# A transformer block in fp32 on one core: layer norm scales of the late half spread by products with the identity, second half's operands split later

## The chip, the core and the metric

The kernel runs on one core of a Trainium2 chip: TensorE (PE) for matmuls, VectorE (DVE), ScalarE (ACT) and GpSimd (POOL) for the rest, and SyncE (SP), which here does nothing but issue DMAs. Each engine takes its instructions in the order of the program and waits, where it must, for semaphores that others raise. The metric is the device time of one execution in microseconds.

## The reference, cut to what matters

```python
x = A_x                                   # 2048 x 1024
h = x + A(layernorm(x), wqkv, w_phi, wo)  # linear attention, 32 heads of 32
h2 = h + relu(layernorm(h) @ w1) @ w2     # w1 1024 x 3584, w2 3584 x 1024
```
A projects to q, k and v, maps q and k per head through w_phi and two softmaxes, sums phi_k^T v and phi_k over all rows, divides, and multiplies by wo. All is fp32. layernorm has no weights: (x - mean) / sqrt(var + 1e-5).

## The kernel before, in words

**Precision.** Each fp32 operand of a large product is split into a high part (`fp32r`, a ScalarE copy) and a low part (the difference, on VectorE or GpSimd), and one product becomes three matmuls, lines L182 to L184 (`mm3`): high by high, high by low, low by high. Three matmuls of 128x512 are one *step*.

**Stages.** In order of the program: the key/value and query projections, the attention, its output projection (`wo`, 32 items of 8 steps: 16 tiles of 128 rows, 2 halves of columns), the up product of the MLP and the down product. Both MLP products are done by a Strassen-like scheme with seven products m in the order 1, 5, 6, 2, 7, 3, 4 (`UP`). The rows come in two halves b = 0 and 1 of 1024. An item (b, p, m) of the up product is 4 steps (12 matmuls); its left operand is a block of w1 (a *unit*), its right one is `hT[m]`, a 128x4x512 operand in a high and a low part, used by 14 items of one half and then overwritten for the other half.

**Where `hT` comes from.** The rows h of tile t are stored to memory (`hd`) by `wo_store` (L688), and their layer norm has two ways. For the first half (*near*, `ln_pair`, i = 0 to 3, two tiles each) a tile is loaded, normed on ScalarE (L239), transposed on TensorE (L246, L715) and copied back by ScalarE (L248, L716); the seven sums are stored to `hs` (L734). The steps of each pair stand in the table `NEAR`. For the second half (*far*, `far_stats`, `far_pair`, table `FAR`) the statistics of each tile are taken as its rows are finished; `ln_power` makes from them two numbers a row (factor and offset, L231 to L233, GpSimd). The rows are loaded later with rows and columns exchanged in another pattern, so that a partition needs the scales of another row: `far_scale` (L748) stores them, four copies of each pair, into memory (`scd`), `far_pair` stage 2 loads them back (L763) into `scx`, and stage 3 norms with them (L769).

**Loading and splitting `hT`.** `h_load` loads `hs` into the low part (L804 for b = 0, L808 for b = 1: g = 0, 1 are the halves of the 512 columns; for b = 1 four DMAs each), `h_high` splits off the high part on ScalarE (L816), `h_low` subtracts on VectorE (L820).

**The up product's results.** After the items m = 1, 5, 6 ScalarE copies the bank (L843, `up_take`), since m = 6, 7, 3, 4 go on summing in a bank that was used before (`BANK_OF`): m = 7 in the bank of m = 6, m = 3 in that of m = 5. VectorE adds (L846, L852, L855), ScalarE takes the relu (L849), and SP stores (L858, `ad`).

**Weights.** The class `Units` loads units (L338, six slots `raw`) and splits them (L125 on ScalarE, L129 on VectorE or GpSimd, ten slots `w`) some steps ahead; a load waits for a slot, that is, for the split of the sixth unit before.

**What sets the order.** There is no scheduler: `when(step, f, ...)` hangs each piece of work on a step, and the text of the program on every engine follows from this. `up_step(b, p, m)` is the step after item (b, p, m); `up0` is the first step of the up product, `wo0` that of the output projection. SP's queue is in order too, and a DMA that waits holds up all behind it.

Of the kernel before, what the change touches and what calls it, by code (L numbers as in the profile page):

```python
# [9 lines left out]
F32 = mybir.dt.float32  # L10
F32R = mybir.dt.float32r
AF = mybir.ActivationFunctionType
# [3 lines left out]
P = 128  # L16
# [6 lines left out]
HT = NT // 2  # L23
NK = D // P
NC = DFF // P
NP = NC // 2
# [114 lines left out]
def kernel(  # L141
# [12 lines left out]
    v, act, pool, pe, sp = nc.vector, nc.scalar, nc.gpsimd, nc.tensor, nc.sync  # L154
# [4 lines left out]
    lnp = ctx.enter_context(tc.tile_pool(name="lnp", bufs=2))  # L159
    dram = ctx.enter_context(tc.tile_pool(name="scratch", bufs=1, space=bass.MemoryType.DRAM))  # L160
# [6 lines left out]
    def tp_bank():  # L167
        return psum.tile([P, 512], F32, name="tp", bufs=2)
# [20 lines left out]
    def do(n, k, f, *args):  # L189
        at[n, k].append((f, args))  # L190
# [9 lines left out]


    hs = {(b, m): dram.tile([P, 4, 4, P], F32, name=f"hs{b}_{m}") for b in range(2) for m in UP}
    scd = [dram.tile([2, 4 * P * 2], F32, name=f"scd{i}") for i in range(4)]
    ad = {(b, m, p): dram.tile([P, 512], F32, name=f"ad{b}_{m}_{p}")
          for b in range(2) for m in UP for p in range(NP)}
    td = {(w, p): dram.tile([P, 4, 512], F32, name=f"t{w}_{p}") for w in (1, 2) for p in range(NP)}
# [2 lines left out]
    xin, xst, xnt = {}, {}, {}  # L209
# [17 lines left out]
    def ln_power(key):  # L227

        mv = xst[key]
        sc = scx[:, key[1] - HT, 0, :] if key[0] == "s" else lnp.tile([P, 2], F32, name="sc", bufs=4)  # L230
        pool.tensor_scalar_add(sc[:, 0:1], mv[:, 1:2], LN_EPS)  # L231
        pool.tensor_tensor(out=sc[:, 0:1], in0=sc[:, 0:1], in1=half, op=ALU.pow)
        pool.tensor_scalar(sc[:, 1:2], mv[:, 0:1], sc[:, 0:1], -1.0, op0=ALU.mult, op1=ALU.mult)  # L233
        xst[key] = sc
# [501 lines left out]
    def far_stats(t, hf):  # L736
        if hf == 0:
            hst[t] = hp.tile([P, 2, 6], F32, name="hst", bufs=8)
        v.bn_stats(out=hst[t][:, hf, :], in_=xh[t, hf])
        if hf == 1:  # L740
            xst["h", t] = mv = lnp.tile([P, 2], F32, name="mv", bufs=4)
            v.bn_aggr(out=mv, in_=hst.pop(t))

    hst = {}

    def far_scale(t):
        dst = scd[t % 4][t % HT // 4].rearrange("(a p s) -> p a s", a=4, s=2)
        sp.dma_start(dst, xst.pop(("h", t))[:, None, :].to_broadcast([P, 4, 2]))  # L748

    def far_swap(dst, src):  # L750
        v.transpose(dst.rearrange("p (c t g) -> p g c t", c=8, g=4), src.rearrange("p (g c k) -> p g c k", g=4, c=8))

    def far_pair(i, stage):

        tiles = [HT + 4 * r + i for r in range(2)]
        if stage < 2:
            t = tiles[stage]
            xnt["h", t] = x = lnp.tile([P, D], F32, name="xin")
            for a in range(4):
                sp.dma_start(x[32 * a:32 * (a + 1)].rearrange("t (g r f) -> t g r f", g=4, r=2),  # L760
                             hd[t].rearrange("(t g) (r a f) -> a t g r f", g=4, r=2, a=4)[a])
        elif stage == 2:
            sp.dma_start(scx[:, 2 * i:2 * i + 2].rearrange("p r g s -> p r (g s)"),  # L763
                         scd[i].rearrange("r (p f) -> p r f", f=8))
        elif stage == 3:
            for r, t in enumerate(tiles):
                for g in range(4):
                    x, sc = xnt["h", t][:, 256 * g:256 * (g + 1)], scx[:, 2 * i + r, g]
                    act.activation(x, x, AF.Identity, bias=sc[:, 1:2], scale=sc[:, 0:1])  # L769
        elif stage == 4:  # L770
            x1, x2 = (xnt.pop(("h", t)) for t in tiles)
            y2 = mp.tile([P, D], F32, name="y2", bufs=1)
            sums[1, i] = x1, x2, y2
            far_swap(y2, x2)
        elif stage == 5:
            s, y1, y2 = sums[1, i]
            far_swap(y1, s)
        elif stage == 6:
            s, y1, y2 = sums[1, i]
            v.tensor_add(s[:, 0:512], y2[:, 0:512], y2[:, 512:])  # L780
            v.tensor_sub(y2[:, 0:512], y1[:, 0:512], y2[:, 0:512])
        elif stage == 7:
            s, y1, y2 = sums[1, i]
            s4 = mp.tile([P, 512], F32, name="s4l", bufs=1)
            pool.tensor_tensor(out=s[:, 512:], in0=s[:, 0:512], in1=y1[:, 0:512], op=ALU.subtract)
            pool.tensor_tensor(out=s4, in0=y1[:, 512:], in1=s[:, 512:], op=ALU.subtract)
            sums[1, i] = s, y1, y2, s4
# [132 lines left out]
    def item(gen, *args, keys):  # L920
        items.append((gen, args + (keys,)))
        steps.extend((k,) for k in keys)
        return len(items) - 1
# [11 lines left out]
    for b, tiles in enumerate(groups):  # L935
        for hf in range(2):

            pairs = b == 0 and hf == 0
            for j in range(0, 4, 2 if pairs else 1):
# [3 lines left out]
                for half in range(2):  # L943
                    n = item(wo_pair, tiles[j:j + 2], hf, half, keys=[("wo", hf, 4 * half + k // 2) for k in range(8)])
# [36 lines left out]
    for t in range(1, NT):  # L981
        n = t - 1 if t < HT else q_n[1, t - HT] + 1
# [107 lines left out]
    for u in range(32):  # L1090
        start = 8 * (a0 + u) if u >= 8 else 8 * (last_kv + 4) + 19 * u // 2
# [10 lines left out]
        if u < EARLY:  # L1102
            start = 8 * (kv_n[1, u // 2, NT - 1] + 4) + (-2, 19)[u % 2]
# [6 lines left out]
    for (t, hf), n in order:  # L1110
        do(max(n - 1, wo_first), -1, wo_load, t, hf)
        added = 8 * n + (11 if n < wo_first + 2 else 9)
        when(added, wo_add, t, hf)
        if t >= HT:
            when(added, far_stats, t, hf)
            if hf == 1:
                when(added + 4, ln_power, ("h", t))
                when(added + 15, far_scale, t)
        when(8 * n + (10 if n > order[-3][1] else 14), wo_store, t, hf)

    NEAR = {1: (0, 9, 12, 17, 30, 31, 32, 33, 35, 40), 2: (6, 14, 17, 20, 24, 25, 26, 27, 29, 36)}
    FAR = 0, 4, 8, 28, 34, 38, 42, 46, 54
    wo0 = 8 * wo_first
    up0 = 8 * first_up
    for i in range(4):
        near, far = wo0 + 64 + 40 * i, up0 + 60 + 68 * i
        ln2 = NEAR.get(i, (0, 9, 12, 17, 24, 25, 26, 27, 29, 36))
        for stage in range(9):  # L1130
            when(near + ln2[stage], ln_pair, i, stage)
        for stage in range(8):
            when(far + FAR[stage], far_pair, i, stage)
        for j in range(7):
            when(near + ln2[9] + j // 2, ln_store, i, j)
            when(far + FAR[8] + j, far_store, i, j)
    assert wo_n[8, 0] + 10 < first_up

    def up_step(b, p, m):

        return up0 + 4 * (up_n[b, p, m] + 1 - first_up)

    for j, m in enumerate(UP):

        for g in range(2):
            step = up0 + (8 * j + (-62, -32)[g] if j < 4 else 6 * (j - 4) + 10 + 2 * g)
            high = up0 + (8 * j + (-48, -19)[g] if j < 4 else 6 * (j - 4) + 20 + 2 * g)
            when(step, h_load, 0, m, g)
            when(high, h_high, m, g)
            when(high + (2 if j < 4 else 5), h_low, m, g)  # L1150
            step = up_step(0, NP - 1, m) + 3 * j
            when(step + 3 * g, h_load, 1, m, g)
            when(step + 13 + 4 * g, h_high, m, g)
            when(step + 16 + 4 * g, h_low, m, g)

    for b in range(2):
        for p in range(NP):
# [10 lines left out]
    for n, (w, p, j) in enumerate((w, p, j) for w in (1, 2) for p in range(NP) for j in range(2)):  # L1168
        step = sums_at[n]
# [26 lines left out]
    scx = consts.tile([P, HT, 4, 2], F32, name="scx")  # L1196
# [5 lines left out]
    ident = consts.tile([P, P], F32, name="ident")  # L1202
# [9 lines left out]
    for i in range(4):  # L1212
        r = slice(32 * i, 32 * (i + 1))
# [76 lines left out]
```

## Time and profile before

| what | value |
|---|---|
| median of 3 runs | 1899.98 us (1899.32 to 1905.49) |
| the profiled execution | 1903.04 us, span 1901.2 us, mean clock 0.994 |
| TensorE busy | 1877.3 us, 99% |
| VectorE, ScalarE, GpSimd busy | 56%, 39%, 51% |
| DMA | 432.24 MB, mean 227 GB/s |
| DMA queue of SP | 413.43 MB, 71.5% of 16 engines' span |

Times are microseconds from the start of the span. A row of a timeline has the start, the length, the engine, the line, the operation, what is written and read, and in brackets how long the engine stood idle before it and what ended that. In the view of waits stand the total, how often, and the longest. SPq is SP's queue.

### The profile page before, as it was taken

The page shows a single profiled execution, that of the slowest core. Times are in us where ns is not written, and L with a number is a line of the kernel's source. Part 1 is how long each engine was busy: PE and PEld are TensorE (multiplying, and loading weights), DVE is VectorE, ACT ScalarE, POOL GpSimd, SP SyncE. Part 2 cuts the span into 40 slices and gives each one's busy share as a digit, 9 for nine tenths or more (in the row PEclk, how much of TensorE's full clock was granted, in tenths as well). Part 3 has the DMA queues.
Part 4 walks back from the last instruction along what each step waited for, and adds up shares of the span by engine and source line. Part 5 has one row for each costly group of instructions (what it writes and reads, how often), then busy time and mean ns, then how long its engine had stood idle before and what let it go on. Part 6 is the DMA issues. An engine that isn't in the chain of part 4 may idle for free.

```text
span 1901.2 us, 31843 instructions
## 1 busy us (share of the span) xinstructions
PE 1877.3 (99%) x11576; PEld 1538.4 (81%) x11576; DVE 1066.5 (56%) x1695; ACT 738.1 (39%) x1270; POOL 971.7 (51%) x959
## 2 busy tenths in 40 slices
PE   9999999999999999989999989999999999999999
PEld 7877788888788888778888878888888888888887
DVE  7777688677689777445555554334433433343333
ACT  5322244222233122345455554444444444444442
POOL 4887744888847898233233222222244444444443
PEclk9999999999999999999999999999999999999999
DMA  7888788666565666997989997566677677767765
GB/s 225 288 289 293 233 293 256 201 193 198 184 211 162 216 233 214 238 214 230 257 255 260 278 247 231 175 193 198 221 240 217 198 234 236 240 210 221 216 215 178
DMA packets 309261, 432.24 MB, mean 227 GB/s; under 512 B 30192, under 2 KB 171504, under 8 KB 309104
## 3 DMA queue, kind: packets, MB, share of 16 engines
q1 hardware_dynamic: 292208, 413.43, 71.5%
q10 hardware_dynamic: 16896, 16.78, 2.6%
q8 instruction: 91, 1.49, 0.3%
q14 instruction: 66, 0.54, 0.1%
HBM read 292.72 MB, written 137.40 MB: 226 GB/s over the span
## 4 chain that ended last, share of the span: by engine, by line
PE 91%; DMA 5%; POOL 2%; SPq 1%; issue 1%; DVE 1%; ACT 0%; ACTq 0%; POOLq 0%; DVEq 0%
PE mm L182 23%; PE mm L183 23%; PE mm L184 23%; PE ac L184 3%; PE ac L183 3%; PE ac L182 3%; DMA hT<-hs 3%; PE tp L184 2%; PE tp L183 2%; PE tp L182 2%; PE tp L246 1%; PE ac L465 1%; PE tp L634 1%; DMA hd<-xh 1%; POOL w L129 1%; PE ac L634 1%
## 5 line engine op out<-in xcount | busy, mean ns | idle before, releaser
L129 POOL TENSOR_TENSOR w<-raw,w 128x512 fp32r<-128x512 f32 x353 | 468.2, 1328 | 741.8 <-ACT w L125 698.6
L125 ACT ACTIVATE w<-raw 128x512 fp32r<-128x512 f32 x686 | 408.5, 626 | 481.0 <-PE mm L184 230.2
L129 DVE TENSOR_TENSOR w<-raw,w 128x512 fp32r<-128x512 f32 x333 | 271.2, 815 | 522.7 <-ACT w L125 519.3
L182 PE MATMUL mm<-w,xT 128*128 128x512 f32 x768 | 305.4, 398 | 0.0
L183 PE MATMUL mm<-w,xT 128*128 128x512 f32 x768 | 299.9, 390 | 0.7 <-POOL w L401 0.4
L184 PE MATMUL mm<-w,xT 128*128 128x512 f32 x768 | 299.3, 390 | 0.0
L182 PE MATMUL mm<-hT,w 128*128 128x512 f32 x672 | 263.6, 392 | 8.0 <-ACT c L843 4.9
L183 PE MATMUL mm<-hT,w 128*128 128x512 f32 x672 | 263.6, 392 | 3.0 <-DVE hT L820 3.0
L184 PE MATMUL mm<-hT,w 128*128 128x512 f32 x672 | 263.1, 392 | 0.0
L363 POOL TENSOR_TENSOR b<-b 128x256 f32<-128x256 f32 x176 | 145.1, 825 | 53.0 <-DMA b<-in_w_dram 38.3
L182 PEld LDWEIGHTS mm<-w,xT 128*128 128x128 f32 x768 | 144.1, 188 | 33.9 <-issue 2.9
L184 PEld LDWEIGHTS mm<-w,xT 128*128 128x128 f32 x768 | 144.2, 188 | 30.7
L183 PEld LDWEIGHTS mm<-w,xT 128*128 128x128 f32 x768 | 144.3, 188 | 30.0 <-POOL w L129 1.0
L182 PEld LDWEIGHTS mm<-hT,w 128*128 128x128 f32 x672 | 127.3, 189 | 35.5 <-ACT c L843 5.3
L182 PE MATMUL mm<-w 128*128 128x512 f32 x392 | 152.5, 389 | 0.0
L183 PE MATMUL mm<-w 128*128 128x512 f32 x392 | 152.5, 389 | 0.0
L184 PE MATMUL mm<-w 128*128 128x512 f32 x392 | 152.5, 389 | 0.0
L183 PEld LDWEIGHTS mm<-hT,w 128*128 128x128 f32 x672 | 127.4, 190 | 30.2 <-DVE hT L820 3.7
L184 PEld LDWEIGHTS mm<-hT,w 128*128 128x128 f32 x672 | 127.3, 189 | 26.4
L183 PEld LDWEIGHTS mm<-w 128*128 128x128 f32 x392 | 73.6, 188 | 15.3
L182 PEld LDWEIGHTS mm<-w 128*128 128x128 f32 x392 | 73.6, 188 | 15.2
L184 PEld LDWEIGHTS mm<-w 128*128 128x128 f32 x392 | 73.6, 188 | 15.2
(177 smaller groups left out, 3144.8 us busy)
## 6 DMA issues: line engine op xcount, KB each, us to landing
raw<-t SPq DMA_DIRECT2D x224, 256.0 KB, 4.0
raw<-ad SPq DMA_DIRECT2D x196, 256.0 KB, 3.0
raw<-in_w_dram SPq DMA_DIRECT2D x168, 256.0 KB, 3.1
ad<-c SPq DMA_DIRECT2D x112, 256.0 KB, 3.8
b<-in_w_dram SPq DMA_DIRECT2D x44, 512.0 KB, 5.8
t<-b SPq DMA_DIRECT2D x44, 512.0 KB, 4.8
ad<-s SPq DMA_DIRECT2D x84, 256.0 KB, 4.1
ed<-qe ACTq DMA_DIRECT2D x32, 512.0 KB, 4.4
```

The source lines that it names most:

```text
L125: nc.scalar.activation(w[:, 0, :], raw[1], AF.Copy)
L129: eng.tensor_tensor(out=w[:, 1, :], in0=raw[1], in1=w[:, 0, :].bitcast(F32), op=ALU.subtract)
L182: pe.matmul(ps, a_hi, b_hi, start=first, stop=False, skip_group_check=more)
L183: pe.matmul(ps, a_hi, b_lo, start=False, stop=False, skip_group_check=more)
L184: pe.matmul(ps, a_lo, b_hi, start=False, stop=last, skip_group_check=more)
L246: pe.transpose(pt[:, k, :], xn[:, (4 * j + k) * P:(4 * j + k + 1) * P], ident)
L363: pool.tensor_tensor(out=tsum[*u, *out], in0=tsum[*u, *a], in1=tsum[*u, *b], op=ALU.subtract)
L465: pe.matmul(kv_ps[s][g][32 * i:32 * (i + 1), 0:64], vt[:, 32 * h:32 * (h + 1)], phi[:, 64 * h:64 * (h + 1)], start=first, stop=last)
L634: pe.matmul(banks[g][32 * c:32 * (c + 1), j * P:(j + 1) * P], kvL[rows, 4 * q + 2 * sd + h // 4, 32 * (h % 4):32 * (h % 4 + 1)], phT_of[u ...
```

## The change

The scales of the second half no longer go through memory. `ln_power` writes them straight into `scx[:, t - 8, 0, :]` (its key is now "f"), and `far_scale`, called once at step `up0 + 26`, multiplies them by columns of the identity: 16 products of 32 x 16 outputs into one bank, which spread the scales of the rows 4t + g to four groups of 32 partitions; one ScalarE copy puts them into `scx`. The eight stores and the four loads are gone, and `far_pair` has a stage less at unchanged steps of the others. Two rows of `NEAR` are changed: pair 1's transposes and sums come a step earlier and its stores three, pair 2's load two steps earlier and its norm and transposes a step later. And the second half's `h_load` comes j steps earlier (j is the place of m in `UP`, 0 to 6), its `h_high` and `h_low` 9 - j steps later.

```diff
-    scd = [dram.tile([2, 4 * P * 2], F32, name=f"scd{i}") for i in range(4)]
...
-        sc = scx[:, key[1] - HT, 0, :] if key[0] == "s" else lnp.tile([P, 2], F32, name="sc", bufs=4)
+        sc = scx[:, key[1] - HT, 0, :] if key[0] in "sf" else lnp.tile([P, 2], F32, name="sc", bufs=4)
...
-    def far_scale(t):
-        dst = scd[t % 4][t % HT // 4].rearrange("(a p s) -> p a s", a=4, s=2)
-        sp.dma_start(dst, xst.pop(("h", t))[:, None, :].to_broadcast([P, 4, 2]))
+    def far_scale():
+        ps = tp_bank()[:, 0:64].rearrange("p (g n s) -> p g n s", g=4, n=HT)
+        for g in range(4):
+            for a in range(4):
+                pe.matmul(ps[32 * a:32 * (a + 1), g], ident.rearrange("p (t g) -> p g t", g=4)[:, g],
+                          scx[:, :, 0, :], start=True, stop=True)
+        act.activation(scx.rearrange("p n g s -> p g n s"), ps, AF.Copy)
...
-            sp.dma_start(scx[:, 2 * i:2 * i + 2].rearrange("p r g s -> p r (g s)"),
-                         scd[i].rearrange("r (p f) -> p r f", f=8))
-        elif stage == 3:
...
-                    x, sc = xnt["h", t][:, 256 * g:256 * (g + 1)], scx[:, 2 * i + r, g]
+                    x, sc = xnt["h", t][:, 256 * g:256 * (g + 1)], scx[:, 4 * r + i, g]
...
-                when(added + 4, ln_power, ("h", t))
-                when(added + 15, far_scale, t)
+                when(added + 4, ln_power, ("f", t))
...
-    NEAR = {1: (0, 9, 12, 17, 30, 31, 32, 33, 35, 40), 2: (6, 14, 17, 20, 24, 25, 26, 27, 29, 36)}
-    FAR = 0, 4, 8, 28, 34, 38, 42, 46, 54
+    NEAR = {1: (0, 9, 12, 17, 29, 30, 31, 32, 34, 37), 2: (4, 14, 17, 21, 25, 26, 27, 28, 30, 36)}
+    FAR = 0, 4, 28, 34, 38, 42, 46, 54
...
+    when(up0 + 26, far_scale)
...
-            step = up_step(0, NP - 1, m) + 3 * j
+            step = up_step(0, NP - 1, m) + 2 * j
             when(step + 3 * g, h_load, 1, m, g)
-            when(step + 13 + 4 * g, h_high, m, g)
-            when(step + 16 + 4 * g, h_low, m, g)
+            when(step + 22 + 4 * g, h_high, m, g)
+            when(step + 25 + 4 * g, h_low, m, g)
```

SP's queue at the first half's last operands, before (`hT_9637` is operand 7, `hT_9638` operand 3; `raw` are units, `scd` the scales):

```order
L688 DMA hd_99<-xh 128x512
L338 DMA raw<-t_2_316 128x512
L338 DMA raw<-t_3_317 128x512
L748 DMA scd_116<-sc 128x4x2
L804 DMA hT_9637<-hs_7_104 128x4x128 x2
L338 DMA raw<-t_2_316 128x512
L804 DMA hT_9637<-hs_7_104 128x4x128 x2
L338 DMA raw<-t_3_317 128x512
L748 DMA scd_117<-sc 128x4x2
L804 DMA hT_9638<-hs_3_105 128x4x128 x4
```
The same place of the changed kernel (`hT_9621` is operand 7, `hT_9622` operand 3):

```order
L687 DMA hd_99<-xh 128x512
L337 DMA raw<-t_2_312 128x512
L337 DMA raw<-t_3_313 128x512
L804 DMA hT_9621<-hs_7_104 128x4x128 x2
L337 DMA raw<-t_2_312 128x512
L804 DMA hT_9621<-hs_7_104 128x4x128 x2
L337 DMA raw<-t_3_313 128x512
L804 DMA hT_9622<-hs_3_105 128x4x128 x4
```
Nothing moved here but that the two stores of scales are gone.

SP's queue where the second half's operands 3 and 4 (`hT_9638`, `hT_9639`) are loaded, before (`ad` are results of the up product):

```order
L338 DMA raw<-t_2_316 128x512
L858 DMA ad_6_13_159<-s_11970 128x512
L858 DMA ad_7_13_187<-c_11956 128x512
L858 DMA ad_3_13_201<-s_11986 128x512
L808 DMA hT_9638<-hs_3_112 32x4x256 x4
L338 DMA raw<-t_3_317 128x512
L808 DMA hT_9638<-hs_3_112 32x4x256 x4
L338 DMA raw<-t_2_316 128x512
L338 DMA raw<-t_3_317 128x512
L808 DMA hT_9639<-hs_4_113 32x4x256 x4
L338 DMA raw<-in_w_dram 128x512
L808 DMA hT_9639<-hs_4_113 32x4x256 x4
```
The same place of the changed kernel (`hT_9622` is operand 3, `hT_9623` operand 4):

```order
L808 DMA hT_9622<-hs_3_112 32x4x256 x4
L858 DMA ad_3_12_196<-s_11945 128x512
L858 DMA ad_5_13_141<-s_11955 128x512
L337 DMA raw<-t_2_312 128x512
L858 DMA ad_6_13_155<-s_11965 128x512
L808 DMA hT_9622<-hs_3_112 32x4x256 x4
L858 DMA ad_7_13_183<-c_11948 128x512
L858 DMA ad_3_13_197<-s_11982 128x512
L337 DMA raw<-t_3_313 128x512
L337 DMA raw<-t_2_312 128x512
L808 DMA hT_9623<-hs_4_113 32x4x256 x8
```
The first four loads of operand 3 stand ahead of six transfers of 256 KB that were ahead of them (of these the rows `ad_3_12` and `ad_5_13` stand above the piece shown of before), the second four ahead of three, and the last four of operand 4 ahead of two.

ScalarE in the same part of the program, before (`c_12063` is the copy after m = 5, p = 1; `c_12087` and `c_12113` those after m = 6, p = 0 and 1; `hT_9638` operand 3 of the second half; `w` the high parts of units):

```order
L843 ACTIVATE c_12063<-mm 128x512
L125 ACTIVATE w<-raw 128x512
L816 ACTIVATE hT_9638<-hT_9638 128x4x256
L843 ACTIVATE c_12087<-mm 128x512
L125 ACTIVATE w<-raw 128x512
L816 ACTIVATE hT_9638<-hT_9638 128x4x256
L843 ACTIVATE c_12113<-mm 128x512
```
The same of the changed kernel (`c_12062`, `c_12083`, `c_12105` are these copies, `hT_9621` and `hT_9622` the operands):

```order
L843 ACTIVATE c_12062<-mm 128x512
L816 ACTIVATE hT_9621<-hT_9621 128x4x256
L125 ACTIVATE w<-raw 128x512
L843 ACTIVATE c_12083<-mm 128x512
L125 ACTIVATE w<-raw 128x512
L816 ACTIVATE hT_9622<-hT_9622 128x4x256
L843 ACTIVATE c_12105<-mm 128x512
L125 ACTIVATE w<-raw 128x512
L816 ACTIVATE hT_9622<-hT_9622 128x4x256
```
Each split of an operand has moved behind one more copy: the copy after m = 6, p = 0 stood behind operand 3's first split and now stands ahead of it.

More of the change, by code (lines that the diff above doesn't have):

```diff
@@ L740, in far_stats @@
         if hf == 1:
-            xst["h", t] = mv = lnp.tile([P, 2], F32, name="mv", bufs=4)
+            xst["f", t] = mv = lnp.tile([P, 2], F32, name="mv", bufs=4)
             v.bn_aggr(out=mv, in_=hst.pop(t))
     hst = {}
-    def far_scale(t):
-        dst = scd[t % 4][t % HT // 4].rearrange("(a p s) -> p a s", a=4, s=2)
-        sp.dma_start(dst, xst.pop(("h", t))[:, None, :].to_broadcast([P, 4, 2]))
+    def far_scale():
[5 more added lines that the diff above has]
+        act.activation(scx.rearrange("p n g s -> p g n s"), ps, AF.Copy)
     def far_swap(dst, src):
@@ L762, in far_pair @@
         elif stage == 2:
-            sp.dma_start(scx[:, 2 * i:2 * i + 2].rearrange("p r g s -> p r (g s)"),
-                         scd[i].rearrange("r (p f) -> p r f", f=8))
-        elif stage == 3:
             for r, t in enumerate(tiles):
                 for g in range(4):
-                    x, sc = xnt["h", t][:, 256 * g:256 * (g + 1)], scx[:, 2 * i + r, g]
+                    x, sc = xnt["h", t][:, 256 * g:256 * (g + 1)], scx[:, 4 * r + i, g]
                     act.activation(x, x, AF.Identity, bias=sc[:, 1:2], scale=sc[:, 0:1])
-        elif stage == 4:
+        elif stage == 3:
             x1, x2 = (xnt.pop(("h", t)) for t in tiles)
@@ L774, in far_pair @@
             far_swap(y2, x2)
-        elif stage == 5:
+        elif stage == 4:
             s, y1, y2 = sums[1, i]
             far_swap(y1, s)
-        elif stage == 6:
+        elif stage == 5:
             s, y1, y2 = sums[1, i]
@@ L781, in far_pair @@
             v.tensor_sub(y2[:, 0:512], y1[:, 0:512], y2[:, 0:512])
-        elif stage == 7:
+        elif stage == 6:
             s, y1, y2 = sums[1, i]
@@ L1131 @@
             when(near + ln2[stage], ln_pair, i, stage)
-        for stage in range(8):
+        for stage in range(7):
             when(far + FAR[stage], far_pair, i, stage)
@@ L1135 @@
             when(near + ln2[9] + j // 2, ln_store, i, j)
-            when(far + FAR[8] + j, far_store, i, j)
+            when(far + FAR[7] + j, far_store, i, j)
     assert wo_n[8, 0] + 10 < first_up
```

## The prediction

> **What bounds the kernel now.** The first page comes first, for the share of TensorE, and then its waits.
>
> ```profile
> PE 1877.3 (99%) x11576; PEld 1538.4 (81%) x11576; DVE 1066.5 (56%) x1695; ACT 738.1 (39%) x1270; POOL 971.7 (51%) x959
> ```
> TensorE is the bound: busy 1877.3 us, 99% of the span of 1901.2 us. A change of order can gain only what TensorE idles, and what it loses at a lower clock afterwards. The view of TensorE's waits is short:
>
> ```profile
> PE mm L182 <- ACT c L843: 4.9, 1, 4.9
> PE tp L715 <- ACT xin L248: 4.1, 1, 4.1
> PE mm L182 <- ACT hT L816: 3.1, 1, 3.1
> PE mm L183 <- DVE hT L820: 3.0, 1, 3.0
> ```
> Each happened once. Third and fourth follow each other directly, so there are three places. The timeline of TensorE puts the middle one at 836 us, and the chain of waits puts the others at 777 and 1112. The table by stretches shows what each costs with its aftermath (columns: length, TensorE busy and count, four engines, granted clock, DMA share, GB/s):
>
> ```profile
> 776.00:787.00 11.00, 6.91 (x23) 5.39 (x22) 2.52 (x3) 2.75 (x5) 2.50 (x2) 0.69 0.96 200
> 835.00:849.00 14.00, 7.93 (x23) 5.80 (x22) 5.89 (x7) 7.28 (x10) 1.79 (x1) 0.76 0.91 236
> 849.00:1064.00 215.00, 215.00 (x950) 178.02 (x949) 117.99 (x142) 110.26 (x195) 66.69 (x48) 1.00 0.88 256
> 1111.00:1122.00 11.00, 6.10 (x18) 4.57 (x17) 3.35 (x4) 4.12 (x6) 0.47 (x1) 0.69 1.10 216
> ```
> The row of 215 us is the measure: 215/950 = 0.226 us for each matmul at full clock. In the three others the mean clock is 0.69 to 0.76 of full speed: after each idle time TensorE runs slower for a while. The first place holds 23 instructions in 11 us, four of them short transposes (0.45 us together by a row below): 11 - 19 x 0.226 - 0.45 = 6.2 us lost, of which 4.1 idle and 2.1 by the clock. The second holds 23 in 14 us: 8.8 us, 6.1 idle and 2.7 by the clock. The third holds 18 in 11 us: 6.9 us, 4.9 and 2.0. Together **22 us, 1.15% of the run**, and that is nearly all that this change can reach.
>
> **Why the first two places wait.** At 777 us ScalarE (in order) stands before the split of an operand (L816), whose load has not landed; behind it stands the copy (L248) that TensorE needs:
>
> ```profile
> 775.15 0.58 ACT L248 ACTIVATE xin<-tp 128x512 f32<-128x512 f32 x1
> 779.62 1.06 ACT L816 ACTIVATE hT<-hT 128x1024 fp32r<-128x1024 f32 x1 [3.89 <-DMA hT<-hs]
> 780.58 1.07 ACT L248 ACTIVATE xin<-tp 128x512 f32<-128x512 f32 x2
> ```
> The SP queue shows what was issued ahead of that load (774.06), and, further down, ahead of the loads of the second place:
>
> ```profile
> 756.84 0.63 SPq L748 DMA_DIRECT2D scd<-sc  x1
> ...
> 760.94 0.84 SPq L748 DMA_DIRECT2D scd<-sc  x1
> ...
> 765.59 8.35 SPq L338 DMA_DIRECT2D raw<-t  x4
> 774.06 1.62 SPq L804 DMA_DIRECT2D hT<-hs  x2
> ```
> ```profile
> 818.27 0.37 SPq L748 DMA_DIRECT2D scd<-sc  x1
> ...
> 821.11 4.39 SPq L338 DMA_DIRECT2D raw<-t  x2
> 825.55 0.43 SPq L748 DMA_DIRECT2D scd<-sc  x1
> 826.07 1.01 SPq L804 DMA_DIRECT2D hT<-hs  x2
> ```
> These small stores of the layer norm scales are the ones that the change removes. The list of DMAs gives their size, and the table by stretches the rate while they are under way:
>
> ```profile
> scd<-sc SPq DMA_DIRECT2D x8, 4.0 KB, 8.7
> ```
> ```profile
> 760.00:766.00 6.00, 6.00 (x86) 4.77 (x75) 3.65 (x9) 1.21 (x4) 1.05 (x3) 1.00 1.15 126
> 766.00:769.00 3.00, 3.00 (x15) 2.49 (x14) 1.50 (x3) 0.00 (x0) 1.03 (x3) 1.00 0.95 320
> 769.00:772.00 3.00, 3.00 (x15) 2.49 (x14) 0.96 (x2) 1.24 (x1) 0.03 (x1) 1.00 1.48 115
> 829.00:835.00 6.00, 6.00 (x29) 4.95 (x28) 0.00 (x0) 0.00 (x0) 1.20 (x1) 1.00 1.14 126
> ```
> 4 KB take 8.7 us to land, and the DMA engines are full (share 0.95 to 1.48) in all four rows, but move 115 to 126 GB/s in three and 320 in the other. At 320 the bytes of the three slow stretches would have taken 6 x 126/320 = 2.4, 1.1 and 2.4 us: 3.6 + 1.9 + 3.6 = 9.1 us are lost there. About four of the eight stores fall in them, so I take **2 us of the whole queue for one store** (an estimate).
>
> **The change part by part.** *Stores and reloads of the scales* (L748, L763): eight stores and four loads go. At the first place two stores stood ahead, in the two slow stretches, worth 3.6 + 1.9 = 5.5 us; the load was 3.9 us late. It lands in time by 1.6 us, and the 6.2 us go. At the second place TensorE lacked the operand for 6.1 us, the third and fourth row of its waits. In the 8 us ahead of the quoted loads two stores were issued (818.27, 825.55): 2 x 2 = 4 us. The rest I expect from the 4.39 us of two raw loads, where SP waits for a slot that ScalarE frees only after another late operand of the same kind. 4 + 4.39 against 6.1 leaves 2.3 us of margin, if that wait goes altogether, and a lack of 2.1 if it stays. I take it that the 8.8 us go. Bounds: nothing of the 15.0 us goes (stores harmless), or all.
>
> *The products with the identity* (16 matmuls of 32 x 16 outputs over 128 rows, one ScalarE copy). No such product is in the trace. Nearest rows: 48 products with 128x32 weights and 64 columns, and the transposes, four of 128x128:
>
> ```profile
> 47.85 0.81 PE ac L465 x48
> ```
> ```profile
> 773.64 0.45 PE tp L246 x4
> ```
> 16 x 0.81/48 = 0.27 us, or 16 x 0.45/4 = 1.8 us. By shape the first is nearest; with 0.1 us for turning from one kind to another I take **0.4 us**, all of it on TensorE's path. They need the scales of the last tile, which GpSimd finishes at
>
> ```profile
> 820.85 0.27 POOL L233 TENSOR_SCALAR sc<-mv,sc 128x1 f32<-128x1 f32 x1
> ```
> TensorE comes to them 26 steps of three matmuls (26 x 0.68 = 17.7 us) after its first product with an operand (814.3):
>
> ```profile
> L182 PE MATMUL mm<-hT,w x672: 387/389/796, 814.3 to 1363.5; 128*128 128x512 f32 x168
> ```
> That is at 832, with 11 us of cover, and behind them everything on TensorE would wait if that cover were gone. The copy lies in ScalarE's idle time, 39% busy.
>
> *Steps of the near pairs 1 and 2.* One step is 0.68 us, earlier for pair 1's transposes and later for pair 2's. Pair 1's norm keeps its step (17), and its transposes now come at 29, 12 steps or 8 us later; pair 2's norm and transposes move together (21 and 25). So nothing new waits, and I cost both at 0, between -0.7 and 0.7 (one step, if TensorE has to wait for it).
>
> *The second half's operands.* ScalarE's timeline before and through the third place:
>
> ```profile
> 1115.36 1.06 ACT L816 ACTIVATE hT<-hT 128x1024 fp32r<-128x1024 f32 x1 [7.55 <-DMA hT<-hs]
> 1116.33 0.58 ACT L843 ACTIVATE c<-mm 128x512 f32<-128x512 f32 x1
> ...
> 1119.39 1.06 ACT L816 ACTIVATE hT<-hT 128x1024 fp32r<-128x1024 f32 x1 [1.96 <-DMA hT<-hs]
> ...
> 1128.00 1.05 ACT L816 ACTIVATE hT<-hT 128x1024 fp32r<-128x1024 f32 x1
> ```
> The copy at 1116.33 frees the bank for operand 7; it stands behind the split of operand 3. By the order of after it comes ahead of that split, so it runs some 8 us sooner (the split's 7.55 us of waiting no longer lie before it), and the wait at 1112 goes. What is late next is the data itself. TensorE's wait of 4.9 us ended with that copy at 1116.9, so it began at 1112.0. Without it operand 3 is due two items of 12 matmuls later, at 1112.0 + 24 x 0.226 = 1117.4, operand 4 at 1122.8. Three transfers of 256 KB fewer stand ahead of operand 3's last quarter loads, two fewer ahead of operand 4's. The stretch is full:
>
> ```profile
> 1064.00:1128.00 64.00, 59.10 (x252) 48.43 (x251) 32.99 (x39) 32.87 (x51) 13.97 (x9) 0.95 1.07 250
> ```
> 256 KB at 250 GB/s are 1.05 us. Operand 3's second split starts at 1119.4 - 3.1 = 1116.3; after 1.06 us on ScalarE and 1.2 on VectorE (the same subtraction of 128x1024) it is whole at 1118.5, 1.1 us late. Operand 4's starts at 1128.0 - 2.1 = 1125.9, is whole at 1128.2, and is due at 1122.8 + 1.1 = 1123.9: 4.3 us late. So 6.9 us go and **5.4 us come**. Bounds: 0 to 10, at 0.05 to 0.1 us of error for each of some 90 transfers ahead.
>
> In the rows the clock falls after 4.1, 6.1 and 4.9 us of idling. [...]
>
> **Sum.** -6.2 - 8.8 - 6.9 + 5.4 + 0.4 = -16.1 us, from the profiled execution's 1903.0 (span 1901.2 and 1.8 around it) to 1886.9. The median of the runs, 1899.98, lies 3.1 us below it; the same gain gives **1884 us**.
>
> **Rivals.** (a) The third place is cleared altogether: for it, the loads come up to 6 steps sooner in the order and the splits 3 to 9 steps later; against it, the full queue above. 1884 - 5.4 = 1878.5. (b) The second place stays in part, because two stores and the slots free less than 6.1 us. For it speaks the lack of 2.1 us if SP's wait for slots stays, against it that what holds these slots is late for the same reason. Half of 8.8 us stays: 1888; all of it: 1893. (c) The change doesn't do what it says: the stores are not what slows the queue, since the rows of 115 and 126 GB/s also hold 512 KB reads of just written rows. Only 6.9 - 5.4 - 0.4 = 1.1 us are left: 1899. [...] (d) Slower: the stalls were also the time in which the DMA queue caught up. TensorE comes 15 us sooner to the second half's loads, and if these don't, the waits there grow to 5.4 + 15 = 20.4 us, spread over four operands, each with 2.3 us by the slower clock (the mean of 2.1, 2.7 and 2.0): 29.6 + 0.4 against 21.9 is 8 us more, 1908. It decides from a backlog of 15 us at 1064. Against it: the DMA share of 0.88 over the 215 us before leaves 26 us free.
>
> **How the numbers follow.** Forecast 0.50, (a) 0.22, (b) 0.13, (c) 0.09, (d) 0.06. What a measurement can tell from no change is 0.3%, 5.7 us: faster is below 1894.3, with forecast, (a) and (b): 0.85. Within: (c), 0.09. Slower: (d), 0.06. The range reaches from (a) with 0.7 us for the pairs and some 2 for its bound, 1876, to (b) whole, 1893.
>
> **What would show it.** Right: no wait of L715 or L182 on ScalarE between 757 and 850, no rate near 120 GB/s there, half the idle time of L816, and at operands 3 and 4 of the second half waits of about 1 and 4 us. Wrong: slow stretches without stores (then (c)); a wait before operand 7 in the first half (b); a wait of TensorE for GpSimd at the new products; waits already before operand 7 in the second half (d).

## The result and the profile after

| what | before | after |
|---|---|---|
| median of the runs on one chip | 1901.59 us (1899.32 to 1905.49) | 1887.6 us (1885.8 to 1889.71) |
| ratio | | 0.9925, 95% interval 0.9902 to 0.9947 |
| the profiled execution | 1903.04 us, span 1901.2 | 1886.22 us, span 1884.4 |
| clock | 0.994 | 0.998 |

The kernel is faster, by 14.0 us between the medians (by the interval of the ratio, 10 to 19 us) and 16.8 us between the profiled spans. The page of the changed kernel, first part, and its view of TensorE's waits:

```profile
PE 1872.2 (99%) x11608; PEld 1535.5 (81%) x11608; DVE 1069.7 (57%) x1695; ACT 739.2 (39%) x1271; POOL 973.2 (52%) x959
```
```profile
PE mm L183 <- DMA ad<-c: 2.2, 1, 2.2
PE mm L182 <- DMA raw<-in_w_dram: 2.0, 1, 2.0
```
The four waits of 3.0 to 4.9 us that led this list before are gone, and two of 2.2 and 2.0 us have come. Their releasers are misleading: no matmul waits for a store of `ad` or for a raw load. The timelines name the real ones. TensorE:

```profile
1108.64 0.79 PE L182 MATMUL mm<-hT,w 128*128 128x512 f32 x1 [1.96 <-DMA raw<-in_w_dram]
1111.62 0.79 PE L183 MATMUL mm<-hT,w 128*128 128x512 f32 x1 [2.19 <-DMA ad<-c]
```
ScalarE and VectorE at that time:

```profile
1107.53 1.06 ACT L816 ACTIVATE hT<-hT 128x1024 fp32r<-128x1024 f32 x1 [1.09 <-DMA hT<-hs]
```
```profile
1109.14 0.69 DVE L129 TENSOR_TENSOR w<-raw,w 128x512 fp32r<-128x512 f32 x1 [2.48 <-ACT w L125]
1109.75 0.68 DVE L846 TENSOR_TENSOR c<-mm,c 128x512 f32<-128x512 f32 x1
1110.35 1.21 DVE L820 TENSOR_TENSOR hT<-hT 128x1024 fp32r<-128x1024 f32 x1
```
The first wait ends where the high part of the second half's operand 4 is whole (1107.53 + 1.06 = 1108.59), the second where its low part is (1110.35 + 1.21 = 1111.56). The low part could have begun at 1108.6, but on VectorE a unit's split and an addition stood ahead.

The table by stretches of the changed kernel, at the places of before (its times run ahead of those of before by up to 15 us after the second place):

```profile
757.00:766.00 9.00, 9.00 (x160) 7.24 (x159) 8.00 (x16) 1.22 (x4) 2.90 (x8) 1.00 0.98 285
...
776.00:787.00 11.00, 11.00 (x52) 9.11 (x51) 8.29 (x10) 5.03 (x8) 6.54 (x4) 1.00 0.42 124
...
829.00:835.00 6.00, 6.00 (x28) 4.95 (x28) 5.02 (x7) 4.84 (x7) 2.37 (x1) 1.00 0.95 270
...
1106.00:1117.00 11.00, 6.85 (x21) 4.79 (x20) 4.97 (x7) 5.65 (x10) 3.06 (x2) 0.69 0.93 298
```
With full DMA engines (shares 0.98 and 0.95) the rate is now 285 and 270 GB/s, where it was 115 to 126. The 124 of the second row is no slow stretch: there the share is 0.42, the engines have little to do. TensorE runs through the first two places without a gap. The third place holds 21 matmuls in 11 us: 11 - 21 x 0.226 = 6.3 us lost, against 6.9 before. ScalarE's idle time before the splits of the operands, which waits for their loads, shrank too:

```profile
ACT hT L816 <- DMA hT<-hs: 27.7, 12, 7.0
```
These are 27.7 us in 12 times; before, the row read 64.7 us in 25 times.

Summed over the start times of all matmuls at full pitch (worked out from the trace's records), the three places lost 7.0, 9.2 and 7.4 us before and 0, 0 and 6.8 us after: 16.8 us.

### The profile page after: what moved, and what is told of

Same layout as the page of the kernel before. It is cut to its first block, busy times and chain, and to the rows that moved or that the text cites. A ratio compares the mean times of both kernels' runs of the same rounds, so it can differ in the third digit from the quotient of the medians.

```text
span 1884.4 us, 31901 instructions
## 1 busy us (share of the span) xinstructions
PE 1872.2 (99%) x11608; PEld 1535.5 (81%) x11608; DVE 1069.7 (57%) x1695; ACT 739.2 (39%) x1271; POOL 973.2 (52%) x959
## 4 chain that ended last, share of the span: by engine, by line
PE 96%; DMA 2%; POOL 1%; DVE 0%; ACT 0%; issue 0%; SPq 0%; POOLq 0%; ACTq 0%
PE mm L182 25%; PE mm L183 24%; PE mm L184 24%; PE ac L182 4%; PE ac L184 4%; PE ac L183 4%; PE tp L184 2%; PE tp L183 2%; PE tp L182 2%; PE tp L245 1%; PE ac L464 1%; PE tp L633 1%; DMA raw<-t 1%; PE ac L633 1%; POOL w L129 0%; DMA ad<-c 0%
## 5 line engine op out<-in xcount | busy, mean ns | idle before, releaser
L184 PEld LDWEIGHTS mm<-w,xT 128*128 128x128 f32 x768 | 144.2, 188 | 30.6
L183 PEld LDWEIGHTS mm<-w,xT 128*128 128x128 f32 x768 | 144.3, 188 | 29.9 <-POOL w L129 1.0
```

The lines of the kernel that those rows point to most:

```text
L183: pe.matmul(ps, a_hi, b_lo, start=False, stop=False, skip_group_check=more)
L184: pe.matmul(ps, a_lo, b_hi, start=False, stop=last, skip_group_check=more)
```

## The experiments

All medians stand beside runs of the kernel before on the same chip; the ratio is to those. The changed kernel's own ratio is 0.9925 (0.9902 to 0.9947). The third place varies between executions: with the same code there, the profiles of two of the kernels below lost 6.8 us in it (`stores_wide`) and 10.3 us (`near_old`), so differences of a few us between single profiles prove nothing there.

**The two halves of the change apart.** In `scales_only` the second half's operands go back to their old steps:

```diff
-            step = up_step(0, NP - 1, m) + 2 * j
+            step = up_step(0, NP - 1, m) + 3 * j
...
-            when(step + 22 + 4 * g, h_high, m, g)
-            when(step + 25 + 4 * g, h_low, m, g)
+            when(step + 13 + 4 * g, h_high, m, g)
+            when(step + 16 + 4 * g, h_low, m, g)
```


> The changed kernel with the second half's loads and splits at the steps of before; only the way of the scales (and the two rows of pair steps) is new. Theory (the scales' stores made the first two places, and the later splits only traded one wait at the third place for another of the same size): 1887 to 1889 us, about the changed kernel's 1887.6; no wait of L715 or L182 on ScalarE between 757 and 850, and the third place back as a wait for the copy L843 of some 5 us. Rival (the later splits gave a good part of the gain): 1893 or more.

Measured: 1886.47 us beside 1901.94, ratio 0.9912 (0.9894 to 0.9930). TensorE's first wait is the old one:

```profile
PE mm L182 <- ACT c L843: 5.2, 1, 5.2
```
`splits_only` is the kernel before with the changed steps of the operands alone (the reverse of the diff above).

> The kernel before with the second half's operands loaded and split at the changed steps; scales through memory as before. Theory: the first two places stay (15 us), the third changes from 6.9 us to about 6.8: 1901.5 us, within 1.5 of the kernel before's 1901.6. Rival (the later splits gave a good part of the gain): 1895 or less.

Measured: 1905.18 us beside 1901.94, ratio 1.0013 (0.9998 to 1.0028). Its waits of TensorE:

```profile
PE mm L182 <- ACT hT L816: 6.4, 2, 3.9
PE tp L715 <- ACT xin L248: 4.1, 1, 4.1
```
The wait of the first place (L715) is as before. The second place is still a wait for an operand, and the third has become one (L816, two times). The time lies 3.2 us above the kernel before, more than the 1.5 us that I had allowed, but the interval holds no change. So the way of the scales gives the whole measurable gain, and the later splits none.

**Is it the stores?** `stores_back` adds to the changed kernel eight stores that nobody reads, in the old pattern and at the old steps; the reloads stay away (lines from L748 on are moved by 5 to 6; the buffers `scd` of the kernel before are there again):

```diff
...
+    def far_spare(t):
+        dst = scd[t % 4][t % HT // 4].rearrange("(a p s) -> p a s", a=4, s=2)
+        sp.dma_start(dst, xst["f", t][:, None, :].to_broadcast([P, 4, 2]))
...
                 when(added + 4, ln_power, ("f", t))
+                when(added + 15, far_spare, t)
```


> The changed kernel with eight more stores of the scales on SyncE's queue, in the pattern of before (512 pieces of 8 bytes each) and at the steps of before; nobody reads them, and nothing else waits for them. Theory (the stores hold up the whole DMA queue by some 2 us each): the rates near 120 GB/s and the stalls of the first two places come back, 1898 to 1903 us. Rival (the stores are harmless; the reloads, SyncE's waits or the moved steps made the difference): 1887 to 1890.

Measured: 1903.15 us beside 1901.94, ratio 1.0001 (0.9988 to 1.0013): the whole gain is gone. The list of DMAs, TensorE's waits and the table by stretches:

```profile
scd<-scx SPq DMA_DIRECT2D x8, 4.0 KB, 9.7
```
```profile
PE mm L182 <- ACT hT L821: 6.1, 2, 4.6
...
PE tp L715 <- ACT xin L248: 3.0, 1, 3.0
```
```profile
760.00:766.00 6.00, 5.44 (x106) 3.98 (x84) 2.35 (x6) 1.21 (x4) 1.03 (x3) 1.00 1.14 146
829.00:835.00 6.00, 6.00 (x57) 4.77 (x56) 0.00 (x0) 0.06 (x1) 0.35 (x1) 1.00 0.93 84
```
84 and 146 GB/s at full engines (0.93 and 1.14), and the waits of both places, with nothing but the stores added. In a full queue they are what costs. (Against what I had expected something does wait for one of them: ScalarE's copy of the scales, which overwrites what the stores read, for 0.8 us. No wait of TensorE names it.)

**What of the stores?** `stores_wide` stores 4 KB at the same places in 8 pieces of 512 bytes:

```diff
...
+    def far_spare(t):
+        sp.dma_start(scd[t % 4][t % HT // 4].rearrange("(p f) -> p f", p=8), ident[0:8])
```


> The changed kernel with eight more stores of 4 KB at the same places, but each in 8 pieces of 512 bytes (of other data). Theory (it is the number of pieces that holds up the queue): no stretch near 120 GB/s and no stall at the first two places, 1887 to 1890 us. Rival (any store there costs, by its place in SyncE's queue or by a fixed cost of one DMA): 1895 or more.

Measured: 1887.52 us beside 1901.94, ratio 0.9921 (0.9899 to 0.9942), with the rate at its height:

```profile
829.00:835.00 6.00, 6.00 (x28) 4.95 (x28) 4.75 (x6) 4.84 (x7) 0.00 (x0) 1.00 0.91 276
```
A store there cost nothing that shows by itself (0.9921, the changed kernel's own 0.9925). `stores_64` has 512 pieces again, each of 64 bytes:

```diff
...
+        dst = scd[t % 4][t % HT // 4].rearrange("(a p s) -> p a s", a=4, s=16)
+        sp.dma_start(dst, ident[:, None, 0:16].to_broadcast([P, 4, 16]))
```


> The changed kernel with eight more stores at the places of before, each again in 512 pieces, but of 64 bytes (32 KB a store, of other data). In the run with the 8-byte pieces the time was 1903.2, with 8 pieces of 512 bytes 1887.5. Theory (the number of pieces holds up the queue): the two stalls come back, 1898 us or more. Rival (it is pieces as small as 8 bytes that hold up what is under way beside them): 32 KB at 320 GB/s are 0.1 us, so 1887 to 1890 and no rate near 120 GB/s.

Measured: 1888.09 us beside 1899.96, ratio 0.9941 (0.9923 to 0.9959):

```profile
scd<-ident SPq DMA_DIRECT2D x8, 32.0 KB, 5.3
```
```profile
829.00:835.00 6.00, 5.07 (x23) 4.13 (x23) 5.43 (x6) 4.42 (x7) 1.31 (x1) 1.00 1.03 290
```
So it isn't the number of pieces either, which I had put first. (TensorE's 5.07 us in this row hold a short wait for an operand, on which more below.) `stores_apart` has the 512 pieces of 8 bytes, each 64 bytes from the next:

```diff
...
+        dst = scd[t % 4][t % HT // 4].rearrange("(a p s) -> p a s", a=4, s=16)[:, :, 0:2]
+        sp.dma_start(dst, xst["f", t][:, None, :].to_broadcast([P, 4, 2]))
```


> The changed kernel with eight more stores at the places of before, each in 512 pieces of 8 bytes, but each piece 64 bytes from the next (in the run with 8-byte pieces side by side the time was 1903.2, with pieces of 64 bytes 1888.1). Theory (a piece of 8 bytes is slow by itself): the stalls come back, 1898 us or more. Rival (the pieces are slow because eight of them fall into the same 64 bytes of memory): 1887 to 1890 us.

Measured: 1890.61 us beside 1901.99, ratio 0.9939 (0.9922 to 0.9956), span 1885.4:

```profile
scd<-scx SPq DMA_DIRECT2D x8, 4.0 KB, 5.2
```
```profile
829.00:835.00 6.00, 5.47 (x25) 4.35 (x24) 5.28 (x6) 3.71 (x6) 1.29 (x1) 1.00 1.05 293
```
The same pieces, at the same places, land in 5.2 us where they took 9.7 side by side, and the rate is 293 GB/s where it was 84. By the medians some 3 of the 15 us are left; the profile is of the fastest of its four runs (1887.16 to 1894.17), so a small cost of the pieces apart is not excluded. The theory that a small piece is slow by itself falls: the stores were slow where eight pieces lay in the same 64 bytes (9.7 us to landing), not where each lay 64 bytes from the next (5.2 us). Only the distances of 8 and 64 bytes were tried, so it is not shown where between them the cost ends, nor whether it is the shared 64 bytes or that a whole store lies within 4 KB, not 32 KB.

**The pairs' steps.** `near_old` is the changed kernel with the two rows of `NEAR` of before.

> The changed kernel with the two rows of pair steps of before. Theory (nothing waits for the moved steps): 1887.6 us, within 0.7. Rival (the moved steps carry a part of the gain at the first place, where the copy after the transposes waited): 1890 or more, with a wait of TensorE between 740 and 790.

Measured: 1887.96 us beside 1899.96, ratio 0.9931 (0.9911 to 0.9951). The stretch where the pairs work:

```profile
740.00:790.00 50.00, 50.00 (x476) 41.15 (x474) 35.01 (x55) 15.43 (x27) 28.04 (x37) 1.00 0.73 227
```
TensorE is never idle in it, so the steps cost and gain nothing that shows.

**The third place.** `load_j1` and `load_j0` load the second half's operands j and 2j steps earlier, with the splits unmoved (`load_j0` has `2 * j` in place of `1 * j`):

```diff
-            when(step + 3 * g, h_load, 1, m, g)
+            when(step - 1 * j + 3 * g, h_load, 1, m, g)
```


> The changed kernel with the second half's operands loaded j steps earlier (operand 4 by 6 steps, 4.1 us; operand 3 by 5), their splits at the same steps. Theory (operand 4 is late because its loads are issued late, and the weight units behind them have time): the waits of 2.0 and 2.2 us before operand 4 and 2.6 us by the clock go, 1881 us, not above 1884. Rival (the queue is full, so the units come late instead): 1887 us or more, with a wait of ScalarE's L125 for a load.

> The same with loads 2j steps earlier (operand 4 by 12 steps, operand 3 by 10): every operand's load begins right after its last use in the first half. Theory as for the loads j steps earlier: the wait before operand 4 goes, 1881 us, unless the units come late: then the time is above that of the loads j steps earlier, up to 1890. Rival (a full queue): no better than 1887.

Measured: 1887.17 and 1890.10 us beside 1899.96, ratios 0.9933 (0.9917 to 0.9948) and 0.9947 (0.9931 to 0.9962). Both miss the 1881 us of my theory; what came is the rival, a full queue in which the units come late instead. With the loads j steps earlier TensorE waits as before, and ScalarE shows why:

```profile
1103.83 0.63 ACT L125 ACTIVATE w<-raw 128x512 fp32r<-128x512 f32 x1 [3.40 <-DMA raw<-t]
...
1106.36 1.04 ACT L816 ACTIVATE hT<-hT 128x1024 fp32r<-128x1024 f32 x1
```
Operand 4's split has no wait of its own any more (no bracket), but it stands behind a unit's split whose load has now come late. What the operand gains in a full queue a unit loses, and in ScalarE's order that unit is first. So three kernels move the operands' splits too. `early_splits`: loads as `load_j1`, operand 4's splits 4 to 5 steps earlier. `early_both`: loads as `load_j0`, those of operands 3 and 4 so:

```diff
-            when(step + 22 + 4 * g, h_high, m, g)
-            when(step + 25 + 4 * g, h_low, m, g)
+            when(step + (18 if j > 4 else 22) + 4 * g, h_high, m, g)
+            when(step + (20 if j > 4 else 25) + 4 * g, h_low, m, g)
```


> The changed kernel with the loads j steps earlier, and operand 4's splits four to five steps earlier, ahead of a unit's split (L125) that waited 3.4 us for its load. Theory (both the loads and the place in ScalarE's queue hold operand 4): the wait falls from 4.9 to about 2 us, since its last loads land at 1106.3 and it is due at 1106.6: 1884 to 1886 us. Rival (the full queue gives the wait back at the units): 1887 us or more.

> The changed kernel with the loads 2j steps earlier and the splits of operands 3 and 4 four to five steps earlier. Theory: the loads land in time and no unit's split stands ahead, the third place goes: 1881 to 1883 us. Rival (the full queue gives the wait back at the units or at another operand): 1887 us or more.

Measured: 1887.05 and 1888.39 us beside 1901.99, ratios 0.9922 (0.9907 to 0.9937) and 0.9928 (0.9911 to 0.9944): no gain, the rival in both. In `early_both` TensorE's wait at the third place, and ScalarE and VectorE at that time, are:

```profile
PE mm L182 <- DVE c L846: 6.5, 1, 6.5
```
```profile
1107.20 0.63 ACT L125 ACTIVATE w<-raw 128x512 fp32r<-128x512 f32 x1 [2.24 <-DMA raw<-t]
1110.32 0.63 ACT L849 ACTIVATE c<-c 128x512 f32<-128x512 f32 x1 [2.49 <-DVE c L846]
1110.86 1.04 ACT L816 ACTIVATE hT<-hT 128x1024 fp32r<-128x1024 f32 x1
```
```profile
1111.93 1.23 DVE L820 TENSOR_TENSOR hT<-hT 128x1024 fp32r<-128x1024 f32 x1 [1.64 <-ACT hT L816]
1113.07 0.68 DVE L846 TENSOR_TENSOR c<-mm,c 128x512 f32<-128x512 f32 x1
```
Operand 4's second split is still behind a unit's on ScalarE (and behind a relu that waits for VectorE). What TensorE waits for in the end is an addition (L846, done at 1113.75): item m = 4 goes on summing in the bank that it reads, and on VectorE it stands behind the operand's low part. In `early_splits` the same addition ends a wait of 3.3 us.

`early_more` (loads as `load_j0`) puts operand 4's splits ahead of both units':

```diff
-            when(step + 22 + 4 * g, h_high, m, g)
-            when(step + 25 + 4 * g, h_low, m, g)
+            when(step + (22, 22, 22, 22, 22, 18, 14)[j] + (3 if j > 5 else 4) * g, h_high, m, g)
+            when(step + (25, 25, 25, 25, 25, 20, 16)[j] + (3 if j > 5 else 4) * g, h_low, m, g)
```


> As the kernel with both earlier, but operand 4's splits four more steps earlier: its high parts now stand ahead of the two units' splits that waited 5.2 and 2.2 us for their loads, its low parts ahead of the additions behind them. In the run before, operand 4's loads had landed at 1101.8, 5.2 us before it was due. Theory (the third place is the order on ScalarE and VectorE, with the loads early enough): it is whole at 1106.2 and the place goes, 1881 to 1883 us. Rival (the queue holds some 4 us too little whatever the order, and the wait only moves on to the units): 1886 us or more, with a wait of TensorE for a unit or an addition behind one.

Measured: 1883.77 us beside 1898.10, ratio 0.9921 (0.9908 to 0.9934); span 1882.1, the lowest, on a chip where the kernel before is fastest too. Waits of TensorE, then ScalarE and VectorE:

```profile
PE mm L182 <- ACT c L849: 2.7, 1, 2.7
```
```profile
1101.96 1.04 ACT L816 ACTIVATE hT<-hT 128x1024 fp32r<-128x1024 f32 x1
...
1106.63 0.63 ACT L125 ACTIVATE w<-raw 128x512 fp32r<-128x512 f32 x1 [3.10 <-DMA raw<-t]
```
```profile
1107.29 0.69 DVE L129 TENSOR_TENSOR w<-raw,w 128x512 fp32r<-128x512 f32 x1 [2.78 <-ACT w L125]
...
1108.50 0.68 DVE L846 TENSOR_TENSOR c<-mm,c 128x512 f32<-128x512 f32 x1
```
Operand 4's last high part is made in time (1103), and TensorE waits all the same, 2.7 us to 1109.3. The last addition above has read the bank of m = 4 at 1108.50 + 0.68 = 1109.2; it stands on VectorE behind a unit's split, whose load ended ScalarE's wait at 1106.6. (The view names L849, which ended at about the same time and doesn't touch the bank. In `early_both` TensorE went on 0.15 us after the addition's end, here 0.14.) The rival was right on the mechanism, and on the time too if it is taken by the ratio: 0.9921 x 1901.59 = 1886.6, not the theory's 1881 to 1883. The place has 4.5 us in this profile, against 6.8. Neither that nor the ratios (0.9921 against 0.9925) show that this kernel is faster than the changed one. That an order with these additions ahead of the units' splits would clear the place was not tried.

## Why the prediction was right

The forecast was 1884 us, from a gain of 16.1 us; measured were 1887.6 by the median, 14.0 us, and 16.8 us between the profiled spans. Step by step:

1. **The three places** and the 22 us: right (23.6 us by the start times). Two of them went, the third stayed as another wait. The first went as forecast, but with a step that I had left out: the four raw loads ahead of the late load (L337, L338 of before) took SyncE 2.08 us, not 8.35, and it issued that load at 764.61, not 774.06:

```profile
762.44 2.08 SPq L337 DMA_DIRECT2D raw<-t  x4
764.61 1.79 SPq L804 DMA_DIRECT2D hT<-hs  x2
```
From issue to landing these loads took no less than before (6.2 us, before 4.9). In `stores_back` the raw loads took SyncE 6.26 us. So the load was late because it was issued late; my 5.5 us for two stores gave the right answer without that step.

2. **The stores hold up the whole queue, about 2 us each:** right, and shown by `stores_back` (all 15 us back) and `stores_wide` (none). Rival (c), harmless stores, is out; the reads of just written rows that it named are still there (one issued at 759.02), at 285 GB/s. The size fits: packets in the stretch 745 to 850 us lasted longer beside them (table below), (116.2 - 97.5) ns x 7413 + (38.0 - 30.4) x 14269 + (440.6 - 237.6) x 256 = 299 us on 16 engines, 18.7 us for eight stores, **2.3 us each** (counted by the DMA engines' time; how that reaches TensorE differs from place to place, see 1 and 3).
3. **The second place:** it went, but not by the way I gave. I expected SyncE's 4.39 us for a slot to go; it stayed:

```profile
811.73 4.24 SPq L337 DMA_DIRECT2D raw<-t  x2
```
By my sum 2.1 us should then have been lacking; that the place went whole is luck as far as my sum goes. What made up for it was the time from issue to landing of the four loads of operand 7, before and after:

```profile
L804 SPq DMA_DIRECT2D hT<-hs x4: 425/448/1214, 826.1 to 828.2; - x4
...
DMA to landing us min/median/max: 8.2/9.2/10.0
```
```profile
L804 SPq DMA_DIRECT2D hT<-hs x4: 385/462/498, 816.1 to 818.1; - x4
...
DMA to landing us min/median/max: 3.6/4.1/6.0
```
They land 9.2 - 4.1 = 5.1 us sooner after their issue (the slowest 4.0), where I had put 4 us on two stores, and SyncE issues them 10.0 us earlier (826.1 to 816.1) while TensorE begins the up product only 7.8 us earlier (814.3 to 806.5; why SyncE gains more is open):

```profile
L182 PE MATMUL mm<-hT,w x672: 389/389/789, 806.5 to 1346.6; 128*128 128x512 f32 x168
```
The margin is smaller than my 2.3 us. Operand 7's low part was whole at 826.40 + 2.35 = 828.75, and TensorE used it at 829.27:

```profile
826.40 2.35 DVE L820 TENSOR_TENSOR hT<-hT 128x1024 fp32r<-128x1024 f32 x2
```
The profiles of two kernels show a wait there: `stores_64` 0.9 us, and `early_splits`, which has no store and the changed kernel's code at that place, 1.0 us. So 0.5 us is within what varies between executions.

4. **The products with the identity:** mis-sized. TensorE's rows around them:

```profile
824.59 0.39 PE L184 MATMUL ac<-hT,w 128*128 128x512 f32 x1
824.91 0.67 PE L749 MATMUL tp<-scx,ident 128*32 128x16 f32 x32
...
825.85 0.39 PE L183 MATMUL ac<-hT,w 128*128 128x512 f32 x1
```
The 16 products stand as 32 records in the trace, and I had misread the row that I went by: its 48 are records too, of 24 products (line L465 makes 512 products, 8 in each of 64 calls, and has 1024 records). By records it gives 32 x 0.81/48 = 0.54 us. The 0.1 us for turning from one kind to another can be read around that row of before:

```profile
47.46 0.40 PE L184 MATMUL mm<-w,xT 128*128 128x512 f32 x1
47.78 0.88 PE L465 MATMUL ac<-kphi,vt 128*32 128x64 f32 x48
48.59 0.50 PE L182 MATMUL mm<-w,xT 128*128 128x512 f32 x1
48.93 0.39 PE L183 MATMUL mm<-w,xT 128*128 128x512 f32 x1
```
The starts lie 0.32 us apart ahead of the 48 records and 0.34 behind them, where one pitch is 0.227: 0.1 us at each side. I had counted it once; with both the row gives 0.54 + 0.2 = 0.74 us. From 824.59 to 825.85 are 1.26 us, where two pitches of 0.227 would stand: 0.8 us, not 0.4, within the bounds. The cover is as computed: GpSimd's last scale (L232) ends at 813.25 + 0.26 = 813.5, 11.4 us ahead.
5. **Pair steps:** 0, as forecast (`near_old`).
6. **The second half's operands:** 6.9 less 5.4 was forecast, 6.9 less 6.3 came (7.4 less 6.8 by the start times). Operand 4's idle time was 1.96 + 2.19 = 4.15 us, and 4.3 had been forecast. That these agree is in part luck. I had it from the landing of the loads alone; but the low part could have been whole at 1108.6 + 1.2 = 1109.8 and was at 1111.56, so some 1.8 us of it came from the order on VectorE. Operand 3, forecast 1.1 us late, was in time. The mis-sized term is the clock, which I had put at nothing although my 6.9 us for the old wait held 2.0 us of it: 6.3 - 4.15 = 2.1 us, 2.6 by the start times. No idle time was as long as the 4.3 us forecast, and yet the clock was at half after the first wait already (the matmul at 1108.64 took 0.79 us) and still so behind the second.

```profile
1111.60:1115.40 3.80, 3.78 (x9) 3.01 (x10) 1.86 (x3) 1.80 (x4) 1.28 (x1) 0.50 1.00 336
```
The sum with the measured terms: -7.0 - 9.2 - 0.6 (7.4 less 6.8) + 0.8 is -16.0; another 0.9 us is the run's opening wait of TensorE for ScalarE, 2.5 us before and 1.6 after, which the change doesn't touch. That makes 16.9 of the 16.8 us. That the four terms sum to -16.0 where I had -16.1 is luck as well: single ones are off by 0.4 to 0.9 us, to both sides. Rivals (a), (b) and (d) did not come: the third place stayed, the second went whole, and the third did not grow.

## What to carry to other kernels

A DMA that is small in bytes can still slow the transfers beside it: here stores of 4 KB, with 84 to 146 GB/s at full engines beside them and 270 to 293 without them or with their pieces apart. Look for stretches where the DMA engines are full and the rate is a third of its best, list what is issued there, and test a suspect by adding it back alone. Before moving a late load ahead, look at what stands ahead of its user on every in-order engine: here the load that fell back was that one's.

## What the runs showed of the hardware

**Neighbouring small pieces.** Packets in the stretch 745 to 850 us, worked out from the DMA records of the traces (mean duration of one, in ns):

| kernel | small pieces of a store | those | 512 B | 2048 B | 4096 B |
|---|---|---|---|---|---|
| after | none | | 30.4 | 97.5 | 237.6 |
| before | 512 of 8 B, side by side | 10.5 | 38.0 | 116.2 | 440.6 |
| stores_back | 512 of 8 B, side by side | 10.7 | 37.6 | 110.0 | 438.3 |
| splits_only | 512 of 8 B, side by side | 15.4 | 39.2 | 111.3 | 442.7 |
| stores_apart | 512 of 8 B, 64 B apart | 9.5 | 30.6 | 96.4 | 205.6 |
| stores_64 | 512 of 64 B | 11.1 | 29.9 | 95.3 | 199.7 |

The pieces themselves cost little side by side or apart: 4096 x 10.5 ns on 16 engines are 2.7 us for all eight stores, 0.34 us each, and 0.5 us in `splits_only`. It is the other packets that get longer, and in these runs only where the pieces lie side by side. Most of them don't: in every row the middle packet of 512, 2048 and 4096 bytes took 27, 84 and 159 ns. Some stall: 307 of these packets took more than 0.5 us in the kernel before, 279 in `stores_back`, and 92 after, 79 in `stores_apart`, 83 in `stores_64`. They make 270 of the 299 us between before and after. The runs show that the stalls come with pieces side by side, not by which part of the memory path.

**Short idle times and the clock.** In `load_j0` TensorE idled 1.17 and 0.98 us (2.15 together), and the matmuls behind took 0.39 us, as ahead:

```profile
1102.51 0.50 PE L182 MATMUL mm<-hT,w 128*128 128x512 f32 x1 [1.17 <-ACT hT L816]
...
1104.00 0.50 PE L183 MATMUL mm<-hT,w 128*128 128x512 f32 x1 [0.98 <-DVE hT L820]
1104.34 0.39 PE L184 MATMUL mm<-hT,w 128*128 128x512 f32 x1
```
In `early_more` it idled 2.67 us, went on at full clock for 1.2 us, and only then slowed, to a mean clock of 0.68 over the stretch:

```profile
1109.32 0.47 PE L182 MATMUL mm<-hT,w 128*128 128x512 f32 x1 [2.67 <-ACT c L849]
...
1110.86 0.63 PE L182 MATMUL mm<-hT,w 128*128 128x512 f32 x1
```
```profile
1108.90:1114.00 5.10, 4.68 (x14) 3.73 (x15) 2.31 (x4) 3.60 (x8) 1.75 (x2) 0.68 0.76 231
```
The slower clock cost 1.7 us there (matmul pitches against 0.227 us). So an idle time of 2.7 us was enough in one run, and two of 1.0 to 1.2 us were free in another. In the changed kernel 1.96 us were enough: its clock record is at half from 1108.68 to 1115.51 us, right after the first wait. In the records of the kernel before and of the changed one each stretch of half clock lasts 6.83 us, but for the last of each, which the run's end cuts. The three of the kernel before (from 780.13, 841.57 and 1114.64) begin 61.44 and 273.07 us apart, 9 and 40 of these lengths, and all three begin while TensorE was still idle (it went on at 781.21, 842.84 and 1116.9). In `early_more` the slow matmuls fill only some 3 us (1110.86 to 1113.85). What sets the length and the beginning, no run tested.
